# Attention and a gelu MLP on one core: q and k of batches 2 to 7 loaded by the casting DMA of GpSimd and transposed in 64-column tiles

## The chip, the core and the metric

The kernel runs on one core of a Trainium2 chip. The metric is the device time of one execution in microseconds, taken as the median of several runs. Beside it, one execution was recorded by the hardware profiler; its span (first to last instruction) is somewhat shorter than its time. The engines are named as in the profile: PE is TensorE's matmul, PEld its weight load, DVE is VectorE, ACT is ScalarE, POOL is GpSimd, SP is SyncE.

## What is computed

The inputs q, k and v have the shape (8 batches, 12 heads, 448 positions, 64); w_in is 768 x 2048 and w_out 2048 x 768. All are float32, and so is the output (3584 x 768).

```python
def _attn_ref(q, k, v) -> np.ndarray:
    S = q.shape[2]
    scale = 1.0 / np.sqrt(q.shape[-1])
    scores = scale * np.matmul(q, k.transpose(0, 1, 3, 2))
    attn = np.maximum(scores, 0.0) ** 2 / S
    return np.matmul(attn, v).astype(np.float32)

def _moe_ref(x, w_in, w_out) -> np.ndarray:
    h = x @ w_in
    g = h * (1.0 / (1.0 + np.exp(-1.702 * h)))
    return (g @ w_out).astype(np.float32)
...
    attn_out = _attn_ref(**attn_kwargs)
    B, H, S, D = attn_out.shape
    x = np.ascontiguousarray(attn_out.transpose(0, 2, 1, 3)).reshape(B * S, H * D)
    return _moe_ref(x=x, **moe_kwargs)
```

## The kernel before

All matmuls run in float16 with float32 sums. The work is cut as follows.

**Attention.** A unit is four heads of one batch: 24 units, three to a batch. For each unit the kernel needs q and k with the head dimension on the partitions (tiles qT and kT), so both are transposed by PE into a PSUM bank and copied out. The scores of a unit come in seven steps of four matmuls each, on 64*64 tiles of PE, into two PSUM banks; a relu on ACT or DVE brings each bank into a tile `at`, a square on ACT or DVE follows in place, and 28 matmuls on 64*64 tiles multiply `at` with v. Their two banks are copied into xb, the input of the MLP.

**MLP.** The product with w_in is done directly for batch 0 (2 matmuls of 448 columns a step). For batches 1 to 7 it is done by Winograd's form of Strassen's scheme with seven products instead of eight (6 matmuls of 224 columns a step), with sums of blocks of w_in (winS) and of xb (T) made by DVE. The result passes through float32 tiles `gf`: a gelu on ACT writes a gf tile, and a widening step on POOL or DVE turns it into float16 in `ring`, which holds the hidden layer of two batches. The product with w_out uses the same seven-product scheme over pairs of 128-token tiles (8 matmuls of 384 columns a step); sums of ring go to `asum`, those of w_out to wT. The results go through `osb` to the output by SP's queue.

**Loads.** v, w_in and w_out, and q and k of units 1 to 5, are loaded by DMAs that GpSimd issues and that convert float32 to float16 on the way (`load_cast`, L98). q and k of unit 0 and of units 6 to 23 are loaded as float32 by SP (`load`, L94) into the tiles qst and kst, of which there is one each, and converted by a copy on POOL, ACT or DVE (`cast`, L103); that copy also lays the columns out in blocks of 128, two heads side by side. Tiles k16 and q16 hold the float16 forms, two buffers each.

**Transposes.** `trans_pe` (L112) has two forms. If the tile was laid out by `cast`, a tensor takes 7 transposes of 128 columns (L117, tile shape 128*128). If it came from `load_cast`, the two halves lie apart, and a tensor takes 14 transposes of 64 columns, with outputs on partitions 0 to 63 and 64 to 127 (L122, tile shape 128*64).

**The order** is written out by hand. A long string of words gives the order of all operations; each engine executes its own in that order, one after another, each waiting for what it needs. A word is a name, its numbers, an optional PSUM bank list after `@`, and an optional engine after `:` (a for ACT, d for DVE, p for POOL). The words used in this text are: `Lq6` (SP load of q of unit 6), `Q6`, `K6` (conversion), `jq1`, `jk1` (casting load by POOL), `V3` (casting load of v of unit 3), `jwa0`, `jwb0` (the two halves of the first piece of w_in), `jo1.0` (a quarter of w_out), `tq6`, `tk6` (transposes), `eq6`, `ek6` (copy out of PSUM), `s5.5` (scores of unit 5, step 5), `r5.5.1` (relu of its second bank, on ACT unless marked), `x5.5` (square, on DVE unless marked), `a5` (product with v), `e5.0` (copy to xb), `f0.4.1` (first product of batch 0, block 4, second of three steps), `g0.4` (its gelu, on ACT), `v0.4` (its widening, on POOL unless marked), `u1.0.0`, `t`, `b` (products, copies and sums of batches 1 to 7), `p`, `h`, `l` (second product and its results), `W`, `S`, `T`, `A` (sums of w_out, w_in, xb and ring), `o` and `q` with numbers (stores), `G3` (a small DMA on SP that waits for the last piece of w_in, L384) and `z` (matmuls on zeros, zp, while the first loads are under way). Default engines stand in this line:

```python
        home = {"K": "a", "Q": "p", "r": "a", "t": "a", "h": "a", "v": "p"}
```

The pools that matter here have these numbers of buffers: k16 and q16 two each, v16 four, gf five, osb three. The eight PSUM banks are named by number in the words, so a step waits until the earlier content of its banks has been read.

Of the kernel before, what the change touches and what calls it, by code (L numbers as in the profile page):

```python
# [8 lines left out]
F32 = mybir.dt.float32  # L9
# [6 lines left out]
def kernel(  # L16
# [31 lines left out]
    for name, bufs in (("cst", 1), ("kst", 1), ("qst", 1), ("k16", 2), ("q16", 2), ("v16", 4),  # L48
                       ("kT", 3), ("qT", 3), ("at", 15), ("xb", 2),
                       ("T1", 1), ("T2", 1), ("T4", 1), ("gf", 5),  # L50
                       ("as0", 1), ("as1", 1), ("osb", 3)):
        pool(name, bufs)
# [10 lines left out]
    gate = const("gate", [1, 64])  # L63
# [30 lines left out]
    def load(n, u):  # L94
        units[u][n + "st"] = new(f"{n}st", [128, 2, S], F32)
        nc.sync.dma_start(out=units[u][n + "st"], in_=quad(n, u))
# [287 lines left out]
    def sp_gate(e, p, i):  # L384
        nc.sync.dma_start(out=gate[0:1, :], in_=win[i][127:128, 0, 0:64])

    with tc.manual_schedule():
# [4 lines left out]
               "G": sp_gate,  # L392
# [29 lines left out]
        def zeros(e, p, n):  # L422
# [8 lines left out]
            "Lq0 Lk0 z9@0 jq1 jk1 I V0 V1 z1 Q0:d z1 z1 z1 z1 z1 z1 tq0@1 K0:d eq0:a tk0@2 ek0 "  # L431
            "tq1@3 jk2 eq1 s0.1@4.5 jq2 s0.4@6.7 s0.5@0.1 r0.1.1 r0.1.0:d s0.0@2.3 jq3 r0.5.1 "
            "r0.5.0:d s0.6@5.4 r0.0.0 r0.0.1:d r0.6.0 s0.2@1.0 x0.5 r0.2.0 s0.3@2.3 tk1@5 r0.2.1 "
            "x0.1 r0.4.0 ek1 jk3 r0.3.0 x0.2 r0.6.1 s1.6@1.0 jwb0 s1.3@6.5 r0.3.1:d r1.6.0 jwa0 "
            "r1.6.1 x0.6 s1.2@2.4 s1.0@3.1 r1.3.0 x0.3 r1.2.0 s1.5@0.6 x0.0 r0.4.1 r1.5.0:d r1.2.1 "
            "s1.1@2.7 r1.0.1 r1.0.0:d tk2@0 r1.1.0 x0.4 s1.4@4.1 r1.3.1 tq2@3 ek2 r1.1.1 a0@2.5 jq4 "
            "eq2 x1.3:a x1.2 jk4 r1.5.1 r1.4.0:d tq3@0 e0.0:a V2 x1.0 s2.3@7.3 e0.1:a tk3@6 jwb2 "
            "eq3 r2.3.1 s2.2@4.2 r1.4.1 ek3 s2.1@5.0 jwa2 r2.3.0 x1.1 s3.3@3.1 r2.1.1 jwa1 s2.4@6.7 "
            "x1.6 r2.2.0 jwb1 x1.4 r3.3.1 x1.5 a1@0.4 r2.1.0 jk5 r2.4.1 r3.3.0:d r2.2.1 jq5 "
            "s2.0@1.5 r2.4.0:d s3.2@7.3 e1.1:a f0.1.0@2 V3 e1.0 r2.0.0 s2.5@6.4 r2.0.1 r3.2.1:d "  # L440
            "jwb3 s3.4@0.1 r3.2.0 f0.1.1 r2.5.1:d r2.5.0 f0.0.0@5 jwa3 x2.2 f0.0.1 r3.4.0 V4 x2.0 "
            "s2.6@3.7 r3.4.1 s3.0@4.6 r2.6.0 x2.1 tk4@0 V5 r3.0.1 f0.2.0@1 r3.0.0:d r2.6.1 jo0.0 "
# [12 lines left out]
            "x5.3 V6 f0.12.0@1 r5.6.1 K6:d f0.14.0@5 v0.4 r5.2.1 f0.12.1 r5.6.0:d Lk7 x5.0:a "
            "u1.1.0@3 x5.1 u1.0.0@2 r5.2.0 x5.6 r5.4.0 f0.13.0@0 x5.5 u1.2.0@7 e4.1:a S3.1 x5.2:a "
            "f0.12.2 x5.4 f0.14.1 g0.12 a5@4.6 S3.3 Q6:d S1.2 Lq8 tq6@1 e5.0:a v0.12:d f0.13.1 T1.1 "
            "e5.1:a f0.14.2 t1.1.0:d tk6@4 g0.14 T1.2 f0.13.2 S0.3 u1.0.1@6 g0.13 S3.2 p0.0@5 "
            "t1.0.0 v0.13 eq6:a b1.0.1 v0.14 S1.4 u1.0.2 ek6:a S3.4 u1.1.1@0 g1.0.1 T1.3 u1.3.0@1 "
            "t1.0.2 b1.1.1 v1.0.1 u1.1.2 S1.3 g1.1.1 u1.0.4 W0.1 t1.1.2 u1.0.3 W2.1 t1.0.4 u1.1.4 "  # L460
            "K7 b1.0.3 u1.1.3 W1.1 g1.0.3 Lk8 f0.9.0@4 T1.4 t1.1.4 u1.0.6 v1.0.3 Q8:a b1.1.3 f0.9.1 "
            "v1.1.1 f0.9.2 b1.0.6 Lq7 u1.1.6 W3.1 g0.9 u1.3.1@6 g1.1.3 b1.1.6 v0.9 t1.2.0 u1.1.5 "
            "v1.1.3:d t1.3.0 A0.1@0 u1.2.1@4 g1.0.6 W2.3 u1.2.2 g1.1.6 v1.0.6 b1.2.1 tk7@0 t1.2.2 "
            "u1.0.5 b1.3.1 v1.1.6 W1.3 u1.3.2 g1.3.1 W0.3 g1.2.1 u1.2.4 v1.3.1 W3.2 t1.3.2 u1.3.3 "
            "t1.2.4 u1.2.3 A0.2@1 ek7:a u1.2.5 W3.3 g1.0.5 b1.2.3 u1.3.4 K8 v1.0.5 h0.0:d tq8@0 "
            "W2.2 u1.2.6 g1.2.5 Lk9 W1.2 eq8:a p0.1@2 v1.2.5 b1.2.6 W0.2 t1.3.4 v1.2.1 W2.4 "
            "s6.0@7.0 p0.2 r6.0.0 Q7 l0.1 g1.1.5 b1.3.3 r6.0.1 V8 s6.4@4.7 Lq9 W0.4 h0.2 s6.2@3.0 "
            "p0.3 A0.3 r6.2.0 r6.4.1 W3.4 r6.2.1 W1.4 r6.4.0 s6.5@3.7 v1.1.5:d tq7@0 r6.5.0 A0.4 "
            "p0.4 r6.5.1 eq7 x6.2:a x6.5 s6.6@4.3 x6.0 h0.4 s6.3@7.0 Q9 r6.6.1 u1.3.5 r6.3.1:d "
            "r6.3.0 tk8@3 l0.3 g1.3.5 p0.5 K9:p Lq10 r6.6.0:d x6.4:a ek8 v1.3.5 Lk11 x6.3:a "  # L470
            "s7.4@0.7 l0.5 s6.1@1.4 u1.3.6 r7.4.0 r6.1.1:d o1 r7.4.1 x6.6 s7.0@3.5 s7.1@0.4 r6.1.0 "
            "p0.6 b1.3.6 r7.0.1 x6.1 r7.1.0 r7.0.0 x7.4 s7.3@7.1 r7.1.1 s7.2@6.5 l0.6 a6@0.3 r7.2.0 "
            "x7.1 o0 r7.3.0 A2.1@0 r7.2.1 s7.6@4.2 x7.0 r7.3.1 s8.4@6.7 V10 tq9@5 r7.6.0 r7.6.1:d "
            "tk9@1 Q10 e6.1:a r8.4.0:d p2.0@4 eq9:a ek9 K11:p r8.4.1:d x7.2:a s8.2@2.3 x7.6 "
            "s7.5@6.5 Lk10 p2.1@1 r7.5.1 r7.5.0:d Lq11 e6.0:a x7.3 x7.5:a r8.2.0:d s8.1@7.5 a7@6.0 "
            "r8.2.1:d r8.1.1 r8.1.0 A2.2@1 h2.0 x8.1 s8.6@2.3 s8.3@5.7 e7.0:a p2.2 r8.3.0:d e7.1:a "
            "K10:p r8.6.0 r8.6.1:d r8.3.1 l2.1 V13 s9.0@6.5 Lk12 x8.6:a s8.0@0.2 x8.3 s8.5@3.7 p2.3 "
            "r8.0.0:d r8.0.1 r9.0.1 x8.2 r8.5.1 x8.0 tk11@0 r8.5.0 u2.1.0@2 x8.4 ek11:a x8.5 a8@5.7 "
# [152 lines left out]
```

## Time and profile before

| | |
|---|---|
| median of 3 runs | 374.8 us (373.97 to 374.81) |
| profiled execution | 374.8 us, span 373.0 us |
| mean granted clock | 0.998 |
| busy share of the span | PE 98%, PEld 68%, DVE 86%, ACT 80%, POOL 31% |
| chain that ended last | PE 95%, DVE 3%, ACT 1% |
| DMA bytes | 43.16 MB, mean 116 GB/s |
| DMA queue of SP | 28.06 MB, 25.7% of 16 engines |
| DMA queue of POOL | 14.09 MB, 25.2% of 16 engines |
| landing of an SP load of q or k (448 KB) | median 4.5 and 4.2 us |
| landing of a POOL load of q or k (224 KB written) | median 5.9 and 5.4 us |

The page gives busy time per engine, then the span in 40 slices, the DMA queues, the chain of work that ended last (followed back from the last instruction to what released each step), the costliest groups of instructions with the idle time ahead of them and what ended it, and the DMA issues. A group line reads: source line, engine, operation, output and inputs, tile shape of PE, sizes, number of instructions, busy us, mean ns of one, idle us ahead and the releaser. A timeline line reads: start us, us, engine, line, operation, tiles, sizes, number, and in brackets the idle time before it and what ended it. PE's matmuls overlap, so the time that one really takes is the distance between the starts of two.

### The profile page before, as it was taken

How to read it: one execution, taken by the hardware profiler on the slowest of the kernel's cores; microseconds unless marked ns; L12 is line 12 of the kernel's file. 1: busy time of each engine (PE TensorE's matmuls, PEld its weight loads, DVE VectorE, ACT ScalarE, POOL GpSimd, SP SyncE). 2: the span in 40 equal slices, each digit the busy share in tenths (PEclk: the TensorE clock that was granted, in tenths of full speed). 3: DMA queues.
4: the chain of work that ended last, by engine and by line, in shares of the span. 5: the costliest groups of instructions: out<-in, count | busy, mean ns of one | idle time of the engine just before them, and what ended most of it. 6: DMA issues, size and time to landing. Idle time of an engine off the chain costs nothing.

```text
span 373.0 us, 9514 instructions
## 1 busy us (share of the span) xinstructions
PE 365.6 (98%) x3830; PEld 252.9 (68%) x3830; DVE 321.5 (86%) x602; ACT 297.3 (80%) x568; POOL 114.3 (31%) x164
## 2 busy tenths in 40 slices
PE   8899999999999999999999999999999999999995
PEld 4444568855589555886568965599568855788663
DVE  3999999999999998898899699978998889767762
ACT  3999989999988999789978997899994897636310
POOL 6464523452334424231341322335400410012000
PEclk9999999999999999999999999999999999999999
DMA  9999999357673437360572524620520301110344
GB/s 195 171 188 206 238 232 232 135 138 203 166 196 99 120 62 209 112 160 2 134 199 34 177 28 114 183 37 2 95 43 2 86 2 41 45 44 16 71 99 114
DMA packets 31981, 43.16 MB, mean 116 GB/s; under 512 B 2368, under 2 KB 28608, under 8 KB 31936
## 3 DMA queue, kind: packets, MB, share of 16 engines
q1 hardware_dynamic: 14928, 28.06, 25.7%
q0 software_dynamic: 16608, 14.09, 25.2%
q8 instruction: 30, 0.49, 0.5%
q10 hardware_dynamic: 400, 0.39, 0.4%
q14 instruction: 15, 0.12, 0.1%
HBM read 45.61 MB, written 11.01 MB: 152 GB/s over the span
## 4 chain that ended last, share of the span: by engine, by line
PE 95%; DVE 3%; ACT 1%; issue 0%
PE ox L188 35%; PE hx L188 30%; PE sc L141 10%; PE av L172 8%; PE ht L208 5%; PE tr L117 4%; PE zp L426 1%; DVE at L85 1%; DVE at L152 1%; PE tr L122 1%; ACT at L154 1%; DVE kT L80 0%; DVE qT L80 0%; DVE osb L357 0%; DVE wT L417 0%
## 5 line engine op out<-in xcount | busy, mean ns | idle before, releaser
L154 ACT ACTIVATE at<-sc 128x448 f16<-128x448 f32 x229 | 112.2, 567 | 10.6 <-PE sc L141 9.9
L198 POOL TENSOR_SCALAR ring<-gf 128x448 f16<-128x448 f32 x87 | 53.7, 617 | 151.0 <-ACT gf L195 144.0
L188 PE MATMUL ox<-wout,ring 128*128 128x384 f16 x448 | 80.3, 326 | 0.0
L188 PEld LDWEIGHTS <-ring 128*128 128x128 f16 x568 | 53.0, 98 | 37.5 <-issue 7.6
L152 DVE TENSOR_SCALAR at<-sc 128x448 f16<-128x448 f32 x107 | 63.9, 617 | 5.8 <-PE sc L141 5.6
L85 DVE TENSOR_TENSOR at<-at 128x896 f16<-128x896 f16 x107 | 65.5, 636 | 1.7 <-ACT at L154 1.6
L188 PEld LDWEIGHTS <-win 128*128 128x128 f16 x672 | 63.8, 98 | 4.4 <-issue 2.1
L85 DVE TENSOR_TENSOR gf<-hx,gf 128x448 f32<-128x448 f32 x84 | 50.8, 620 | 9.9 <-PE hx L188 5.2
L160 ACT ACTIVATE at<-at 128x896 f16<-128x896 f16 x61 | 57.7, 960 | 0.5
L188 PE MATMUL hx<-xb,win 128*128 128x224 f16 x504 | 57.0, 259 | 0.0
L195 ACT ACTIVATE gf<-gf 128x448 f32<-128x448 f32 x84 | 47.2, 578 | 11.5 <-DVE gf L85 11.3
L141 PE MATMUL sc<-qT,kT 64*64 64x448 f16 x672 | 50.2, 359 | 1.6 <-DVE kT L80 1.1
L188 PEld LDWEIGHTS <-winS 128*128 128x128 f16 x504 | 48.0, 98 | 3.1 <-issue 1.3
L76 ACT ACTIVATE gf<-hx 128x448 f32<-128x448 f32 x60 | 31.8, 541 | 13.4 <-PE hx L188 11.4
L188 PE MATMUL ox<-wT,asum 128*128 128x384 f16 x224 | 40.6, 327 | 0.0
L188 PE MATMUL hx<-T,winS 128*128 128x224 f16 x336 | 39.7, 259 | 0.0
L172 PE MATMUL av<-at,v 64*64 64x448 f16 x672 | 36.2, 350 | 0.1
L141 PEld LDWEIGHTS <-kT 64*64 64x64 f16 x672 | 17.1, 105 | 23.9 <-issue 17.3
L188 PEld LDWEIGHTS <-asum 128*128 128x128 f16 x224 | 20.8, 98 | 16.6 <-issue 3.4
L357 DVE SCALAR_TENSOR_TENSOR osb<-ox,osb 128x384 f32<-128x384 f32 (+1 forms) x44 | 23.8, 541 | 5.9 <-PE ox L188 5.7
L78 ACT ACTIVATE osb<-ox 128x384 f32<-128x384 f32 x26 | 13.1, 503 | 19.6 <-PE ox L188 16.8
L172 PEld LDWEIGHTS <-v 64*64 64x64 f16 x672 | 20.4, 107 | 11.6 <-issue 1.5
(61 smaller groups left out, 426.0 us busy)
## 6 DMA issues: line engine op xcount, KB each, us to landing
out_dram<-osb SPq DMA_DIRECT2D x52, 192.0 KB, 3.0
qst<-in_q_dram SPq DMA_DIRECT2D x19, 448.0 KB, 4.5
kst<-in_k_dram SPq DMA_DIRECT2D x19, 448.0 KB, 4.2
v<-in_v_dram POOLq DMA_DIRECT2D x24, 224.0 KB, 5.0
win<-in_moe_w_in_dram POOLq DMA_DIRECT2D x8, 384.0 KB, 9.7
wout<-in_moe_w_out_dram POOLq DMA_DIRECT2D x4, 768.0 KB, 20.6
q<-in_q_dram POOLq DMA_DIRECT2D x5, 224.0 KB, 5.9
k<-in_k_dram POOLq DMA_DIRECT2D x5, 224.0 KB, 5.4
```

The source lines that it names most:

```text
L76: nc.scalar.activation(out=o, in_=i, func=AF.Copy)
L85: eng[e].tensor_tensor(out=o, in0=x, in1=y, op=op)
L141: nc.tensor.matmul(out=sc[a][c, 0:S], lhsT=st["kT"][r, j, c], rhs=st["qT"][r, :, c], start=True, stop=True)
L152: nc.vector.tensor_scalar(out=o, in0=i, scalar1=0.0, scalar2=None, op0=ALU.max)
L154: nc.scalar.activation(out=o, in_=i, func=AF.Relu)
L160: nc.scalar.activation(out=at, in_=at, func=AF.Square)
L172: nc.tensor.matmul(out=av[s][64 * a:64 * a + 64, 0:S], lhsT=v16[r, a, 64 * j:64 * j + 64], rhs=at[r, a, :], start=(j == 0), stop=(j == J - 1))
L188: nc.tensor.matmul(out=o, lhsT=lhs(i), rhs=rhs(i), start=start and i == 0, stop=i == n - 1, skip_group_check=True)
L195: nc.scalar.activation(out=o, in_=i, func=AF.Gelu_apprx_sigmoid, scale=1.0 / SC)
L198: eng[e].tensor_scalar(out=o, in0=i, scalar1=SC, scalar2=1.0, op0=ALU.mult, op1=ALU.mult)
L208: nc.tensor.matmul(out=hp[g, f][:, 0:S], lhsT=w[:, i, fo:fo + 128], rhs=xts[g][:, i, :], start=i == 0, stop=i == NK - 1)
L357: nc.vector.scalar_tensor_tensor(out=o, in0=x, scalar=1.0 / SC, in1=o, op0=ALU.mult, op1=ALU.add)
```

## The change

q and k of units 6 to 23 (batches 2 to 7) are no longer loaded by SP as float32 and converted. They are loaded by POOL's casting DMA, as those of units 1 to 5 were, and are transposed in the 64-column form. Only unit 0 keeps the float32 load, now into a piece of `ring` that is not yet in use. The tiles qst and kst go, k16 and q16 have four buffers each, and G3 with its tile goes. All operations stand in a new order; the number of every other operation stays the same, and a few steps change between ACT, DVE and POOL. In the diff only the beginning of the two orders is shown, up to the first Strassen steps of batch 1.

```diff
@@ -45,7 +45,7 @@
     def pool(name, bufs, **kw):
         pools[name] = ctx.enter_context(tc.tile_pool(name=name, bufs=bufs, **kw))
 
-    for name, bufs in (("cst", 1), ("kst", 1), ("qst", 1), ("k16", 2), ("q16", 2), ("v16", 4),
+    for name, bufs in (("cst", 1), ("k16", 4), ("q16", 4), ("v16", 4),
                        ("kT", 3), ("qT", 3), ("at", 15), ("xb", 2),
                        ("T1", 1), ("T2", 1), ("T4", 1), ("gf", 5),
                        ("as0", 1), ("as1", 1), ("osb", 3)):
@@ -60,7 +60,6 @@
         return pools["cst"].tile(shape, dt, name=name)
 
     ident = const("ident", [128, 128])
-    gate = const("gate", [1, 64])
     warm = const("warm", [1, 1], F32)
     win = [const(f"win{i}", [128, NK, WQ * 128]) for i in range(NF // WQ)]
     winS = [[const(f"winS{i}_{n}", [128, HK, 256]) for n in range(3)] for i in range(NF // WQ)]
@@ -92,7 +91,9 @@
         return src[n][b].rearrange("(a i s) (p j) d -> i (s p) a (j d)", a=2, i=NP, j=J)[pr]
 
     def load(n, u):
-        units[u][n + "st"] = new(f"{n}st", [128, 2, S], F32)
+        o = "kq".index(n) * 4 * S
+        x = ring.rearrange("p f c -> p (f c)")[:, o:o + 4 * S].bitcast(F32)
+        units[u][n + "st"] = x.rearrange("p (a c) -> p a c", a=2)
         nc.sync.dma_start(out=units[u][n + "st"], in_=quad(n, u))
 
     def load_cast(n, u):
@@ -381,15 +382,11 @@
             in_=moe_w_out[i * WO * 128:(i + 1) * WO * 128, h * NOUT:(h + 1) * NOUT].rearrange(
                 "(f p) d -> p f d", p=128))
 
-    def sp_gate(e, p, i):
-        nc.sync.dma_start(out=gate[0:1, :], in_=win[i][127:128, 0, 0:64])
-
     with tc.manual_schedule():
         two = {"S": s_sum, "W": w_sum, "T": t_sum, "s": scores, "r": relu, "x": square,
                "e": xt_evac, "f": m1, "o": store, "u": unit_product,
                "t": unit_snap, "b": unit_add, "A": a_sum, "p": pair_product, "h": pair_snap,
                "l": pair_last, "q": store_part, "jo": load_w_out, "a": attn_v,
-               "G": sp_gate,
                "I": lambda e, p: make_identity(nc, ident),
                "jwa": lambda e, p, i: load_w_in(0, i), "jwb": lambda e, p, i: load_w_in(1, i),
                "V": lambda e, p, u: load_cast("v", u)}
@@ -428,175 +425,172 @@
 
         two["z"] = zeros
         words = (
-            "Lq0 Lk0 z9@0 jq1 jk1 I V0 V1 z1 Q0:d z1 z1 z1 z1 z1 z1 tq0@1 K0:d eq0:a tk0@2 ek0 "
-            "tq1@3 jk2 eq1 s0.1@4.5 jq2 s0.4@6.7 s0.5@0.1 r0.1.1 r0.1.0:d s0.0@2.3 jq3 r0.5.1 "
-            "r0.5.0:d s0.6@5.4 r0.0.0 r0.0.1:d r0.6.0 s0.2@1.0 x0.5 r0.2.0 s0.3@2.3 tk1@5 r0.2.1 "
-            "x0.1 r0.4.0 ek1 jk3 r0.3.0 x0.2 r0.6.1 s1.6@1.0 jwb0 s1.3@6.5 r0.3.1:d r1.6.0 jwa0 "
-            "r1.6.1 x0.6 s1.2@2.4 s1.0@3.1 r1.3.0 x0.3 r1.2.0 s1.5@0.6 x0.0 r0.4.1 r1.5.0:d r1.2.1 "
-            "s1.1@2.7 r1.0.1 r1.0.0:d tk2@0 r1.1.0 x0.4 s1.4@4.1 r1.3.1 tq2@3 ek2 r1.1.1 a0@2.5 jq4 "
-            "eq2 x1.3:a x1.2 jk4 r1.5.1 r1.4.0:d tq3@0 e0.0:a V2 x1.0 s2.3@7.3 e0.1:a tk3@6 jwb2 "
-            "eq3 r2.3.1 s2.2@4.2 r1.4.1 ek3 s2.1@5.0 jwa2 r2.3.0 x1.1 s3.3@3.1 r2.1.1 jwa1 s2.4@6.7 "
-            "x1.6 r2.2.0 jwb1 x1.4 r3.3.1 x1.5 a1@0.4 r2.1.0 jk5 r2.4.1 r3.3.0:d r2.2.1 jq5 "
-            "s2.0@1.5 r2.4.0:d s3.2@7.3 e1.1:a f0.1.0@2 V3 e1.0 r2.0.0 s2.5@6.4 r2.0.1 r3.2.1:d "
-            "jwb3 s3.4@0.1 r3.2.0 f0.1.1 r2.5.1:d r2.5.0 f0.0.0@5 jwa3 x2.2 f0.0.1 r3.4.0 V4 x2.0 "
-            "s2.6@3.7 r3.4.1 s3.0@4.6 r2.6.0 x2.1 tk4@0 V5 r3.0.1 f0.2.0@1 r3.0.0:d r2.6.1 jo0.0 "
-            "f0.2.1 x2.3 x2.5:a s3.6@3.6 x2.4 x2.6 a2@4.7 jo1.0 r3.6.0 r3.6.1 jo1.1 x3.4 tq4@3 ek4 "
-            "e2.0:a jo0.1 f0.3.0@6 e2.1:a x3.0 f0.3.1 x3.2:a S0.1 f0.0.2 V14 f0.3.2 S0.2 g0.0 "
-            "f0.1.2 eq4 g0.3 f0.2.2 g0.1 x3.3 s3.1@0.4 v0.3 s4.3@7.5 g0.2 s4.1@3.6 v0.1:d f0.10.0@2 "
-            "r4.1.1 f0.10.1 r3.1.1:d r4.3.0 f0.10.2 r3.1.0 v0.0:d f0.8.0@1 r4.3.1 f0.8.1 x3.1 g0.10 "
-            "f0.8.2 v0.2:d r4.1.0 s4.6@6.4 S2.1 v0.10 s4.5@7.0 s3.5@5.2 r4.5.0:d r4.5.1 f0.4.0@3 "
-            "g0.8 f0.4.1 r4.6.0:d f0.6.0@7 x3.6:a v0.8:d f0.4.2 r3.5.1:d f0.6.1 r4.6.1 x4.5 f0.6.2 "
-            "r3.5.0 x4.1 tq5@0 g0.4 tk5@1 x3.5 g0.6 s4.2@6.2 eq5:a ek5 s4.4@4.5 a3@3.7 r4.4.1:d "
-            "r4.2.0 G3 x4.3 r4.2.1 Lk6 s4.0@0.1 S1.1 s5.0@5.6 e3.1:a Lq6 f0.5.0@2 r4.0.0:d r4.4.0 "
...
+            "Lq0 Lk0 z9@0 jq1 jk1 jq2 jk2 jq3 z1 Q0:d z1 z1 I z1 z1 z1 z1 V0 tq0@1 K0:d eq0:a jwa0 "
+            "tk0@2 jk3 ek0 tq1@3 eq1 V1 s0.4@4.5 s0.2@6.7 s0.0@0.1 r0.4.0 r0.4.1:d s0.6@2.3 jq4 "
+            "r0.2.0 r0.0.1:d s0.5@4.5 r0.2.1 jwb0 x0.4 r0.5.0 s0.1@6.1 tk1@7 r0.6.1:d r0.1.0 V2 "
+            "tq2@4 r0.6.0 x0.2 jk4 s0.3@3.6 r0.1.1 ek1 r0.5.1 jwa2 eq2 r0.0.0 s1.6@2.1 s1.0@7.5 "
+            "r0.3.0:d r1.6.0 jq5 s1.1@4.0 r1.6.1 x0.0 tk2@3 jwb2 r1.0.0 r1.0.1:d s1.2@2.1 r1.1.1 "
+            "jwb1 ek2 r0.3.1 tq3@7 x0.6 r1.2.1 jk5 s1.4@5.0 s1.5@3.6 r1.1.0 r1.4.1:d jwa1 r1.5.1 "
+            "r1.4.0:d s1.3@1.4 x0.1:a V3 x1.0 x0.3 x0.5 a0@0.6 r1.2.0 jwb3 r1.5.0 jwa3 eq3:a x1.2 "
+            "s2.3@5.2 x1.4 r1.3.0 V4 s2.5@3.7 e0.0:a r1.3.1:d tk3@1 e0.1:a jo0.0 x1.1 s2.2@0.4 "
+            "r2.3.0 ek3 r2.5.0 s2.4@6.5 x1.6 x1.3:a x1.5 a1@1.3 r2.4.0 r2.4.1:d r2.3.1 r2.2.0:d "
+            "r2.2.1 s2.0@6.5 V5 e1.0 f0.1.0@2 e1.1:a s2.6@0.4 r2.5.1 r2.0.1:d s3.3@1.3 jq6 r2.6.1 "
+            "f0.1.1 r2.0.0:d r3.3.0 f0.0.0@7 jo1.0 x2.4 r2.6.0 s2.1@5.4 s3.4@6.1 x2.2 r2.1.0 jo1.1 "
+            "f0.0.1 r2.1.1 r3.3.1:d f0.3.0@0 f0.3.1 r3.4.0 jk6 x2.1 r3.4.1 s3.0@5.4 s3.2@3.6 x2.0 "
+            "jq8 r3.0.1 tq4@1 r3.2.0:d r3.2.1 tk4@4 jo0.1 x2.5:a x2.3 x2.6 a2@3.6 jk7 r3.0.0 ek4 "
+            "eq4:a jq7 f0.2.0@5 e2.1 f0.2.1 e2.0:a V6 x3.4 s4.5@4.1 s3.6@6.3 r4.5.0:d r4.5.1 f0.3.2 "
+            "r3.6.0 f0.2.2 r3.6.1:d f0.0.2 g0.3 x3.0 f0.1.2 g0.2 s4.3@4.1 g0.0 s4.1@6.3 v0.2 "
+            "s3.5@0.5 r4.3.0:d r4.1.0 f0.8.0@7 v0.0 r4.1.1:d r3.5.1 f0.8.1 f0.10.0@4 g0.1 jk8 x4.1 "
+            "f0.8.2 x3.6:a S0.1 f0.10.1 f0.10.2 x3.2 r3.5.0 s4.0@6.3 v0.3:d r4.3.1 s3.1@5.2 "
+            "r4.0.0:d tk5@0 r3.1.1 tq5@1 g0.10 ek5 f0.6.0@6 r3.1.0 S2.1 f0.6.1 g0.8 x3.3 f0.6.2 "
+            "r4.0.1 f0.4.0@2 v0.8 eq5 x3.1:a f0.4.1 x3.5 jk9 f0.4.2 x4.0 s4.2@4.0 g0.4 s4.6@5.7 jq9 "
+            "a3@3.1 S2.2 g0.6 v0.4 r4.2.0:d r4.2.1 r4.6.1 v0.10 s5.5@2.6 s5.0@4.0 e3.1 r5.5.1 v0.6 "
+            "f0.7.0@7 r5.0.1:d r5.5.0 f0.7.1 v0.1 f0.7.2 e3.0:a r5.0.0:d r4.6.0 s4.4@1.6 V8 S1.1 "
+            "s5.4@0.2 s5.1@3.4 r4.4.0 x4.2 f0.12.0@5 r4.4.1 f0.15.0@1 x4.6 g0.7 f0.12.1 x4.4 r5.4.0 "
+            "f0.12.2 r5.1.1 S1.2 f0.15.1 r5.1.0 f0.11.0@6 S2.4 f0.15.2 x4.3:a r5.4.1:d f0.11.1 S1.3 "
+            "f0.11.2 g0.12 f0.14.0@7 x4.5 g0.15 s5.3@0.4 x5.1 a4@3.2 v0.15 r5.3.1 S3.1 g0.11 v0.12 "
+            "r5.3.0 s5.6@5.1 S3.2 s5.2@4.6 f0.5.0@0 v0.11 r5.2.1 r5.6.1:d f0.5.1 r5.2.0 f0.13.0@6 "
+            "x5.3 V7 e4.0:a f0.5.2 x5.4 x5.2:a f0.14.1 r5.6.0:d u1.0.0@1 x5.0:a S0.2 u1.1.0@4 S3.3 "
+            "f0.13.1 x5.5:a x5.6 a5@3.5 v0.7:d e4.1:a S1.4 g0.5 t1.1.0:d tq6@2 v0.5 e5.0:a T1.1 "
...
```

## The prediction

> **What bounds the kernel now.** I read the page first, then busy time by stretches, the chain of waits in order of time, TensorE's groups with shapes kept apart, and GpSimd's and ScalarE's timelines where the first transfers crowd.
>
> The page's busy times, then two stretches (columns: us, busy us of PE, PEld, DVE, ACT and POOL with instruction counts, clock, DMA share, GB/s):
>
> ```profile
> PE 365.6 (98%) x3830; PEld 252.9 (68%) x3830; DVE 321.5 (86%) x602; ACT 297.3 (80%) x568; POOL 114.3 (31%) x164
> ```
> ```profile
> 0.00:23.00 23.00, 20.19 (x255) 10.85 (x256) 17.22 (x34) 17.08 (x36) 14.36 (x26) 1.00 1.07 183
> 23.00:60.00 37.00, 37.00 (x412) 21.12 (x413) 35.41 (x70) 34.89 (x71) 15.15 (x21) 1.00 1.24 223
> ```
>
> PE never rests from 23 us on: its start-to-start times sum to the span there. So every nanosecond added to PE's stream after 23 us is added to the kernel, and every wait of PE too; freed DVE, ACT or POOL time is worth nothing by itself. Note the DMA share above 1 until 60 us: the 16 DMA engines are full all that while.
>
> Pieces of the chain (start us, us, what), and the two transpose forms (the last figures: busy us, mean ns, idle):
>
> ```profile
> 37.88 0.90 PE tr L122 x28
> ...
> 72.46 1.30 PE ox L188 x8
> 74.07 1.41 PE ox L188 x8
> ...
> 123.68 0.78 PE tr L117 x14
> ```
> ```profile
> L117 PE MATMUL tr<-ident,q 128*128 128x128 f16 x133 | 10.6, 219 | 0.0
> L122 PE MATMUL tr<-ident,q 128*64 128x128 f16 x70 | 2.9, 222 | 0.0
> ```
>
> A tensor turned by 7 full-width transposes (L117) takes 0.39 us; by 14 of 64 columns (L122), 28 to 30 ns apart, 0.415 us, plus something when the next work has another tile shape. The same 8 matmuls take 1.30 us when the next work also uses 128*128 tiles and 1.41 when it is a score (64*64). Start to start over all steps, a change of tile shape costs 0.094 us.
>
> GpSimd, 24 to 40 us, then ScalarE's gelus into gf in those us:
>
> ```profile
> 24.14 0.68 POOL L375 DMA_DIRECT2D win<-in_moe_w_in_dram  x1 [0.49 <-DMA v<-in_v_dram]
> 27.00 0.66 POOL L375 DMA_DIRECT2D win<-in_moe_w_in_dram  x1 [2.18 <-DMA win<-in_moe_w_in_dram]
> 28.90 0.71 POOL L100 DMA_DIRECT2D v<-in_v_dram  x1 [1.24 <-DMA win<-in_moe_w_in_dram]
> ...
> 36.72 0.88 POOL L379 DMA_DIRECT2D wout<-in_moe_w_out_dram  x1 [0.22 <-issue]
> 38.79 0.70 POOL L100 DMA_DIRECT2D v<-in_v_dram  x1 [1.20 <-PE tr L122]
> 39.56 1.46 POOL L198 TENSOR_SCALAR ring<-gf 128x448 f16<-128x448 f32 x2
> ```
> ```profile
> 35.83 0.54 ACT L195 ACTIVATE gf<-ht 128x448 f32<-128x448 f32 x1
> ...
> 37.94 1.00 ACT L195 ACTIVATE gf<-ht 128x448 f32<-128x448 f32 x2
> ```
>
> The issue of a casting DMA waits for an earlier one to land. In the trace the 22nd to the 29th were issued at 27.00, 28.90, 30.88, 32.64, 34.75, 35.62, 36.72, 38.79; the 14th to the 21st landed at 26.72, 28.61, 30.35, 32.35, 34.47, 35.10, 36.43, 38.26. So eight may be under way: number n goes about 0.3 us after number n-8 has landed, and all that stands behind it on POOL waits too. The first widen of batch 0 on POOL (v0.3), placed among PE steps of 32 us, therefore ran at 39.56. It cost nothing: v0.1, v0.0, v0.2 and v0.8 are on DVE, and the gelus g0.8, g0.4, g0.6 (35.83, 37.94 and after) found free gf buffers without POOL.
>
> **The change part by part.** *Transposes.* 36 tensors go from L117 to L122: 36 x (0.415 - 0.391) = 0.9 us. *Order.* Walking both orders, PE changes tile shape 136 times before and 151 times after (the new order puts 20 pairs of transposes back to back, but they now differ from everything around them): 15 x 0.094 = 1.4 us. All other PE steps are the same in number and shape. So PE gains 2.3 us; bounds: 0.9 if no change of shape were added, 4.3 if each tensor took the 0.51 us of the chain's single pieces. Counted with these durations from f0.1.0 (22.93 us in before) PE would end at 366.3 before (it really ended at 368.4) and 369.1 after: 2.9 us, of which 0.5 is work that the new order puts behind f0.1.0.
>
> A rule of the Trainium skill speaks against the 64-column form: "TensorEngine Tiling", Restrictions, says that column tiling turns fast weight load off, and "TensorE: Matmul & The Clock Gate", LDWEIGHTS, prices a load at its columns over 1.2 GHz, 53 ns for 64; were these loads the limit, a tensor would take an estimated 0.75 us and the change cost 13 us on PE. The trace has 28 to 30 ns between these transposes, so the loads overlap, and the row is used.
>
> *Casts.* 36 casts go: on POOL 12 of 1.145 and 13 of 0.976 us (26.4), on ACT 7 of 0.95 (6.7), on DVE 4 of about 0.65 (2.6). POOL gets 36 more issues at 0.75 (27.0), so its sum is unchanged. ACT and DVE are not the bound after 23 us; taken at nothing, hidden under PE's unbroken stream. What this could at most return is the 2.1 us that PE loses in before against its own count. *SP* loses 36 loads and the gate behind win3; its stores no longer queue with loads: nothing waits for them. *Landing.* A cast load took 5.4 to 5.9 us against 4.2 to 4.5; after batch 1 each stands at least 11 us of PE work ahead of its transpose. Nothing.
>
> *Head.* Up to f0.1.0 ACT has 15.6 us of work after and 16.1 before, DVE 16.0 in both, and both are busy almost without a gap from 8.3 us: no change. The identity is now behind five issues (1.26 + 0.89 + 4 x 0.72 = 5.0, ready 5.6), still before tq0 at 6.20.
>
> *What POOL is held up by.* This is the large term. Before the first widen the new order has 34 casting DMAs instead of 29: V6 is the 34th, and waits for the 26th. The first 21 of before are, but for their order, in the first 26 of after, with five more: a w_in piece (384 KB, 2.0 us between landings), V4 and V5 (1.15 each), jo0.0 (a w_out quarter, 768 KB) and jq6 (1.17). For w_out I take 3.8: twice w_in is 4.0; four of them with four SP loads (1.57 each) took from 42.32 to 63.24, giving 3.65. With the 1.65 us that before lost between its 4th and 5th landing to a two-deep buffer, the 26th lands at 38.26 + 2.0 + 2.3 + 3.8 + 1.2 - 1.65 = 45.9. V6 goes at 46.2 and ends at 46.9; v0.2 ends at 47.5, v0.0 at 48.1 (0.6 each). Then k8 waits for jo1.0 (49.7), so v0.8 ends at 51.3; k9 for jo1.1 (53.5), q9 for jk6 (54.7), ending at 55.7; then v0.4, v0.10, v0.6, v0.1 end at 56.3, 56.9, 57.5, 58.1.
>
> Now only one early widen is on DVE (v0.3). gf has five buffers: g0.3, g0.2, g0.0, g0.1, g0.10 take them, g0.8 gets v0.3's, g0.4 must have v0.2's and g0.6 v0.0's. ACT, in order, stands at g0.4 until 47.5, with r4.2.1, r4.6.1 and the rest queued behind. PE's count reaches s5.5 at 40.7; its banks 2 and 6 come free with g0.4 and g0.6, at 48.7: 8.0 us lost. Then g0.7 takes v0.8's buffer in time, but g0.12, g0.15, g0.11 need v0.4, v0.10, v0.6 (56.3, 56.9, 57.5); s5.6 needs the banks of the first two, s5.2 that of the third, and f0.5.0 the relu r5.3.0 behind them, at about 58.9 where the count says 49.0. Lag 9.9 us. By then the w_out quarters have landed (the last about 60) and no later DMA is that long; PE, the bound, gives nothing back. If POOL's landings are 2 us earlier, the lag is some 7; if gf were handed out in strict rotation, g0.7 would wait for v0.1 and f0.5.0 come at 63.5, lag 14.5.
>
> *Clock.* The opening 16 zp matmuls (128x384) took 5.24 us, 0.32 apart, where the same width later takes 0.163: a PE that was idle starts at half pace. An 8 us rest may bring that back, for 0 to 2.6 us. From 48.7 to 57.5 PE has 7.8 us of work in 8.8, so at most 1.6 would show. I take 0. The skill's clock page ("TensorE: Matmul & The Clock Gate", Part 1: The HAM clock gate) puts the drop after about 3.4 us of idleness and the recovery at as much, so by it an estimated 1.7 us would be lost and at most 0.7 show.
>
> Sum, against the profiled execution (374.8 us, span 373.0; also the median): 374.8 + 2.9 + 9.9 = 387.6.
>
> **The rivals.** (a) *POOL is not held up where it hurts*: the gelus find buffers, and only PE's 2.9 us remain: 377.7 (376.3 to 379). For it: before lived with a POOL 8 us late. Against it: then four of the first six widens were on DVE, now one. (b) *Strict rotation of gf* and the half clock: 374.8 + 2.9 + 14.5 = 392.2, to 393.8. Against it: in before g0.6 did not wait for v0.3. (c) *Faster, by the head*: PE takes 16.7 us from tq0 to f0.1.0 for 11.2 us of work. POOL waited 2.4, 1.6 and 3.4 us there for its two k16 and q16 buffers; with four, tensors come earlier. If that returned 5 us and POOL's lateness hurt nobody, 374.8 + 2.9 - 5 = 372.7; it decides if f0.1.0 starts before 20.0 us. Against it: ACT and DVE have no gap there for it to close.
>
> **How the numbers follow.** Held up as worked out, 383 to 393: 0.66. Held up for less (lag 2 to 5, 379 to 383): 0.09. (a): 0.14. (b): 0.05. (c): 0.06. The range leaves out the upper end of (b), (c) and the lower part of (a): 377.0 to 392.5. About 0.3% (1.1 us) is what a measurement of this kernel can tell. Faster by more than that: (c), 0.06; within it: the lowest of (a), 0.03; slower: 0.91.
>
> **What would show it.** Right: 644 transposes of form 128*64 at about 30 ns and 28 of the other; POOL's waits name wout and k DMAs between 38 and 56 us, its first widen ends near 47.5; ACT's gelu waits for POOL's ring widen; PE has a hole of some 8 us near 41 and a second, shorter one near 57; the rest as before, PE's last matmul near 381. Wrong: a first POOL widen near 40, or gelus that pass it; PE without a hole; transposes above 50 ns apart; f0.1.0 moved by more than 2 us.

## The result, and the profile after

The changed kernel takes 386.69 us, the median of three runs (385.88 to 386.87). The ratio to the kernel before, 374.8 us, is 1.0319, with a 95% interval of 1.0288 to 1.035. The forecast was 387.6 us, slower. The profiled execution took 386.87 us with a span of 385.1 us.

The page's busy times come first, then the same two stretches as before and a finer cut of the second one. The columns of a stretch are us, busy us of PE, PEld, DVE, ACT and POOL with instruction counts, granted clock, DMA share and GB/s.

```profile
PE 370.5 (96%) x4082; PEld 254.1 (66%) x4082; DVE 326.1 (85%) x610; ACT 287.5 (75%) x551; POOL 114.5 (30%) x173
```
```profile
0.00:23.00 23.00, 20.19 (x256) 10.95 (x256) 17.49 (x34) 17.39 (x35) 15.05 (x27) 1.00 1.12 201
23.00:60.00 37.00, 29.01 (x306) 13.53 (x299) 25.81 (x47) 25.13 (x52) 17.90 (x25) 0.86 1.29 203
```
```profile
23.00:41.00 18.00, 17.48 (x218) 8.73 (x211) 16.81 (x32) 15.18 (x31) 8.09 (x11) 1.00 1.28 202
41.00:48.30 7.30, 0.00 (x0) 0.00 (x0) 0.17 (x1) 0.55 (x1) 3.31 (x6) 0.65 1.30 203
48.30:60.00 11.70, 11.53 (x88) 4.80 (x88) 8.82 (x15) 9.41 (x20) 6.50 (x10) 0.78 1.30 204
60.00:106.00 46.00, 46.00 (x541) 31.89 (x540) 44.51 (x86) 40.00 (x79) 18.31 (x26) 1.00 0.55 88
```

The first 23 us and everything from 60 us on look as they did: PE is never at rest from there. Between 23 and 60 us PE starts 306 matmuls where it started 412. For 7.3 us it starts none, while DVE and ACT stand almost still too and the DMA engines stay full. What works in those 7.3 us are the transfers and POOL.

More than a few steps changed their engine with the new order: some 360 of the 1100 steps for which the order chooses among ACT, DVE and POOL, nearly as many one way as the other. Among them are seven widens of batch 0 (v0.0, v0.1, v0.2, v0.6, v0.8, v0.11, v0.12) that went from DVE to POOL. As the experiments show, the slowdown comes from these together with the loads, not from the loads alone.

GpSimd's timeline and then ScalarE's, where the loads crowd (start us, us, engine, line, operation, tiles, number; in brackets the idle time ahead and what ended it):

```profile
43.78 0.70 POOL L101 DMA_DIRECT2D k<-in_k_dram  x1 [2.67 <-DMA wout<-in_moe_w_out_dram]
45.22 0.70 POOL L101 DMA_DIRECT2D q<-in_q_dram  x1 [0.74 <-DMA v<-in_v_dram]
46.33 0.70 POOL L101 DMA_DIRECT2D v<-in_v_dram  x1 [0.41 <-issue]
47.11 1.21 POOL L199 TENSOR_SCALAR ring<-gf 128x448 f16<-128x448 f32 x2
```
```profile
47.71 1.19 ACT L196 ACTIVATE gf<-ht 128x448 f32<-128x448 f32 x2 [9.14 <-POOL ring L199]
...
56.92 0.54 ACT L196 ACTIVATE gf<-ht 128x448 f32<-128x448 f32 x1 [0.48 <-POOL ring L199]
```

POOL's first two widens run from 47.11 to 48.32, behind the issue of V6, as forecast (v0.2 done at 47.5, v0.0 at 48.1). ScalarE stands for 9.14 us at g0.4 until a gf buffer is widened. The line of 56.92 is the forecast's second, shorter hold-up, at g0.12 (then g0.15 and g0.11). TensorE, in the next fence, waits 7.80 us for g0.4 and g0.6 to free the banks of s5.5:

```profile
39.00 1.49 PE L173 MATMUL av<-at,v 64*64 64x448 f16 x28
48.30 1.67 PE L142 MATMUL sc<-qT,kT 64*64 64x448 f16 x8 [7.80 <-ACT gf L196]
49.90 2.42 PE L209 MATMUL ht<-xb,win 128*128 128x448 f16 x6
```

The chain of waits puts the same stretch down to a transfer. It has a piece there that the chain of before did not have, the landing of a v tile (V5), which the issue of jq7 at 45.22 waited for:

```profile
30.91 13.78 DMA v<-in_v_dram
```

The transposes, by form (the last figures: busy us, mean ns, idle us):

```profile
L123 PE MATMUL tr<-ident,q 128*64 128x128 f16 x322 | 13.0, 220 | 0.1
L118 PE MATMUL tr<-ident,q 128*128 128x128 f16 x7 | 0.6, 219 | 0.0
```

With those of k that is 644 of the 64-column form, as forecast, still 0.415 us from a tensor's first transpose to the next step of the same tile shape. The forecast's 28 of full width is a wrong count: unit 0 has two tensors of 7, so there are 14. No term of the sum rests on it.

### The profile page after: what moved, and what is told of

It reads as the page before. It is cut to its first block, busy times and chain, and to the rows that moved or that the text cites. A ratio compares the mean times of both kernels' runs of the same rounds, so it can differ in the third digit from the quotient of the medians.

```text
span 385.1 us, 9956 instructions
## 1 busy us (share of the span) xinstructions
PE 370.5 (96%) x4082; PEld 254.1 (66%) x4082; DVE 326.1 (85%) x610; ACT 287.5 (75%) x551; POOL 114.5 (30%) x173
## 3 DMA queue, kind: packets, MB, share of 16 engines
q0 software_dynamic: 26400, 22.35, 39.6%
## 4 chain that ended last, share of the span: by engine, by line
PE 89%; ACT 4%; DMA 4%; DVE 1%; issue 1%; POOL 0%; POOLq 0%
PE ox L189 34%; PE hx L189 30%; PE sc L142 9%; PE av L173 7%; PE tr L123 5%; DMA v<-in_v_dram 4%; ACT at L155 3%; PE ht L209 3%; PE zp L423 1%; DVE at L84 1%; ACT at L161 0%; POOL ring L199 0%; ACT gf L196 0%; DVE winS L84 0%; ACT qT L75 0%
## 5 line engine op out<-in xcount | busy, mean ns | idle before, releaser
L155 ACT ACTIVATE at<-sc 128x448 f16<-128x448 f32 x230 | 113.5, 567 | 11.9 <-PE sc L142 11.3
L153 DVE TENSOR_SCALAR at<-sc 128x448 f16<-128x448 f32 x106 | 62.9, 617 | 13.3 <-PE sc L142 12.9
L84 DVE TENSOR_TENSOR at<-at 128x896 f16<-128x896 f16 x108 | 67.2, 639 | 2.3 <-ACT at L155 1.4
L142 PE MATMUL sc<-qT,kT 64*64 64x448 f16 x672 | 51.6, 365 | 9.0 <-ACT gf L196 7.8
L142 PEld LDWEIGHTS <-kT 64*64 64x64 f16 x672 | 18.0, 106 | 32.9 <-issue 26.4
L173 PE MATMUL av<-at,v 64*64 64x448 f16 x672 | 37.0, 350 | 0.5 <-ACT at L161 0.5
L101 POOL DMA_DIRECT2D v<-in_v_dram x24 | 17.3, 721 | 37.4 <-PE sc L142 31.4
```

Of the source, the lines that this page charges most:

```text
L84: eng[e].tensor_tensor(out=o, in0=x, in1=y, op=op)
L142: nc.tensor.matmul(out=sc[a][c, 0:S], lhsT=st["kT"][r, j, c], rhs=st["qT"][r, :, c], start=True, stop=True)
L153: nc.vector.tensor_scalar(out=o, in0=i, scalar1=0.0, scalar2=None, op0=ALU.max)
L155: nc.scalar.activation(out=o, in_=i, func=AF.Relu)
L173: nc.tensor.matmul(out=av[s][64 * a:64 * a + 64, 0:S], lhsT=v16[r, a, 64 * j:64 * j + 64], rhs=at[r, a, :], start=(j == 0), stop=(j == J - 1))
```

## The experiments

The first four ran together on one chip, beside a kernel before of 375.12 us (374.23 to 375.41). They take the two parts of the slowdown apart: POOL's lateness and PE's dearer transposes.

**The ten early widens on DVE.** The order of the changed kernel is kept, and POOL's queue with all its loads; only ten widens of batch 0 leave it.

```diff
-  ... v0.2 ... v0.0 ... v0.8 ... v0.4 ... v0.10 ... v0.6 ... v0.1 ... v0.15 ... v0.12 ... v0.11
+  ... v0.2:d ... v0.0:d ... v0.8:d ... v0.4:d ... v0.10:d ... v0.6:d ... v0.1:d ... v0.15:d ... v0.12:d ... v0.11:d
```

> The changed kernel with ten early widens of batch 0 (v0.2, v0.0, v0.8, v0.4, v0.10, v0.6, v0.1, v0.15, v0.12, v0.11) on DVE instead of POOL; every load, its place and PE's stream stay. Theory (widens stand behind waiting DMAs on POOL): the hole of 8 us near 41 us goes, and the second near 57. PE's own count gives 377.7; DVE takes on ten widens of about 0.4 us where it was 95% busy, of which 0 to 4 us may show: 379.5 us expected, 377.5 to 382. Rival (the loads land too late for PE, or the transposes are dear): nothing of that changes, 385 to 387.

Measured: 378.47 us (377.92 to 378.62), ratio 1.0089 (1.0074 to 1.0104). POOL's timeline shows that the loads are as late as ever, and the waits of ScalarE for POOL's widens (us in all, count, longest) have gone from 12.4 us, the longest 9.1, to next to nothing:

```profile
42.67 0.70 POOL L101 DMA_DIRECT2D k<-in_k_dram  x1 [2.97 <-DMA wout<-in_moe_w_out_dram]
...
45.83 0.70 POOL L101 DMA_DIRECT2D v<-in_v_dram  x1 [1.03 <-PE ht L209]
```
```profile
ACT gf L196 <- POOL ring L199: 2.4, 5, 0.8
```

So the late loads by themselves hurt nobody. What costs is that widens stand behind them in POOL's queue.

**The loads behind the widens.** The other way round: the widens stay on POOL, and eight loads of units 6 to 9 move behind them.

```diff
-  ... jk6 ... jq8 ... jk7 ... jq7 ... V6 ... jk8 ... jk9 ... jq9 ... v0.1 ... V7 ... v1.0.5
+  ... v0.1 V6 ... V7 jk6 ... v1.0.1 jk7 ... v1.1.1 jq8 ... v0.13 jq7 ... v1.0.3 jk8 ... v1.1.3 jk9 ... v1.0.5 jq9
```

> The changed kernel with eight casting loads (V6, k6, q8, k7, q7, k8, k9, q9) moved in the order behind the early widens of batch 0; engines and PE's stream stay. Theory: the first widen on POOL is then behind 29 casting DMAs as in the kernel before, runs near 38 us, and ACT does not stand: 377.9 us, 376.8 to 379.5. Rival (DVE and ACT were short of time in the new order, or the transposes cost 8 us or more): 384 or more.

Measured: 378.96 us (378.16 to 379.11), ratio 1.0101 (1.0084 to 1.0118), 1.1 us above what was expected. POOL's first widen now runs here:

```profile
37.92 2.25 POOL L199 TENSOR_SCALAR ring<-gf 128x448 f16<-128x448 f32 x3
```

The long hole is gone without any help from DVE. Four small ones remain in PE's stream, of 1.11 us (a3), 0.65 (s5.5), 0.88 (u1.2.4) and 0.48 (tk7), which the expectation did not have. Two edits that have nothing in common but the order of widens and loads on POOL each take about 8 us away.

**The kernel before, transposed in 64-column tiles.** Order, loads and conversions are those of before; the converted tensors of units 6 to 23 are turned by 14 transposes.

```diff
-            if len(x.shape) == 2:
+            if len(x.shape) == 2 and u == 0:
...
+                w = (x[:, a, 64 * j:64 * j + 64] if len(x.shape) == 3
+                     else x[:, 128 * j + 64 * a:128 * j + 64 * a + 64])
...
-                    lhsT=x[:, a, 64 * j:64 * j + 64], rhs=ident[:, :], is_transpose=True)
+                    lhsT=w, rhs=ident[:, :], is_transpose=True)
```

> The kernel before with one thing changed: q and k of units 6 to 23 are transposed in 14 pieces of 64 columns (tile shape 128*64) instead of 7 of 128; loads, conversions and order stay. By the count of the trace before, 36 x 0.024 us and 47 more changes of tile shape (183 against 136) x 0.094 us: +5.3, 380.1 us expected, 379 to 381. Rival by the weight-load rule (53 ns for each of 504 loads): +13 or more, 388. Rival that changes of shape hide: +0.9, 375.7.

Measured: 380.39 us (380.33 to 380.59), ratio 1.0144 (1.0129 to 1.0159): 5.27 us above before, where the count says 5.3. The page's busy line has PE at work for 5.6 us more than before's 365.6, and for the same share of the span, so this is PE's own work:

```profile
PE 371.2 (98%) x4082; PEld 251.5 (66%) x4082; DVE 324.6 (86%) x602; ACT 298.4 (79%) x568; POOL 112.2 (30%) x164
```

In before's order the 64-column form raises the changes of tile shape from 136 to 183, and these 47 at 0.094 us make 4.4 of the 5.3 us. The new order, with its pairs of transposes back to back, has only 151. The Trainium skill's rule on the lost fast weight load ("TensorEngine Tiling", Restrictions), priced by "TensorE: Matmul & The Clock Gate", LDWEIGHTS, would by an estimate have made this run some 13 us slower; the measured 5.27 us speak against it.

**The kernel before with the cast loads.** Before's order again, with the 64-column form, and now also with POOL's casting loads in the places of SP's; the conversions and G3 go, and k16 and q16 have four buffers. The first two new loads, q6 and k6, stand between the w_out pieces; they alone of the new loads come ahead of the first widen.

```diff
-  ... Lk6 ... Lq6 ... K6:d ... Q6:d ... Lq8 ... K7 ...
+  ... jo1.0 jq6 jo1.1 jk6 ... jq8 ...
```

> The order of the kernel before with the loads of the change: q and k of units 6 to 23 by POOL's casting DMA into four buffers each, at the places of the SP loads (q6 and k6 moved up between the w_out quarters), the conversions and the gate gone, 64-column transposes. PE's stream is that of the kernel before with 64-column transposes. Theory: in this order four of the first six widens are on DVE, so the two more DMAs ahead of the first POOL widen hurt nobody, and the time is that of the kernel before with 64-column transposes within 1 us: 380, 379 to 381.5. Rival (the casting loads themselves cost the time, in any order): 8 us or more above that kernel, 388.

Measured: 379.24 us (379.02 to 379.7), ratio 1.0111 (1.0094 to 1.0128). POOL's first widen is about 1 us later than before's 39.56, and PE has no hole:

```profile
40.70 1.49 POOL L202 TENSOR_SCALAR ring<-gf 128x448 f16<-128x448 f32 x2
```

It takes 1.15 us less than the run before it (0.63 in the two profiled executions). That is all that the freed conversions return, net of what the new loads cost; the dearer transposes cost more than four times as much. Little of it reaches PE: its last matmul ends at 374.07 us, against 374.03 in the run before. From f0.1.0 on PE is 0.6 us quicker, but f0.1.0 comes at 23.32 instead of 22.70. What is left is the end, where 3.8 us follow PE's last matmul instead of 4.5.

The next four ran beside a kernel before of 374.43 us (374.1 to 376.11).

**The changed kernel again.**

> The changed kernel as it is, for a comparison on the same chip as the next three: 386.7 us, 385.5 to 388.

Measured: 386.34 us (386.17 to 386.91), ratio 1.0311 (1.0284 to 1.0338). Its profile shows how far two executions of one kernel differ inside: the landings come some 0.8 us earlier (the 26th at 44.92 us instead of 45.80), the wait ahead of s5.5 is 6.4 us instead of 7.8, and f0.5.0 starts at 59.02 instead of 59.74.

**Two widens on DVE.** Only v0.2 and v0.0, which held g0.4 and g0.6 up. If the loss were the hole at 41 us, this would return nearly all of it.

```diff
-  ... v0.2 ... v0.0 ...
+  ... v0.2:d ... v0.0:d ...
```

> The changed kernel with only the first two POOL widens (v0.2, v0.0) on DVE. Theory (the lag is set by the latest of the absolute times at which POOL gets to its widens, not by the sum of PE's holes): the hole of 8 us before s5.5 goes, but g0.7 then stands until v0.8 (about 51 us) and g0.12, g0.15, g0.11 until v0.4, v0.10, v0.6 (56.5 to 58.6), so f0.5.0 still starts near 59 us (59.7 in the changed kernel) and the time is 386.0, 384.5 to 387. Rival (each hole is a cost of its own): 8 us come back, 378.5.

Measured: 387.56 us (387.09 to 388.11), ratio 1.0341 (1.0313 to 1.037), 1.2 us more than the changed kernel beside it and 0.6 above the expected range. PE's and then ScalarE's timelines show the hole moved to the next widens in POOL's queue:

```profile
51.87 0.91 PE L209 MATMUL ht<-xb,win 128*128 128x448 f16 x2 [5.54 <-ACT gf L196]
```
```profile
51.27 0.54 ACT L196 ACTIVATE gf<-ht 128x448 f32<-128x448 f32 x1 [7.80 <-POOL ring L199]
```

v0.8 is behind jk8, and v0.4 and its neighbours behind jk9 and jq9, as POOL's timeline shows:

```profile
49.90 0.70 POOL L101 DMA_DIRECT2D k<-in_k_dram  x1 [2.90 <-DMA wout<-in_moe_w_out_dram]
50.68 0.56 POOL L199 TENSOR_SCALAR ring<-gf 128x448 f16<-128x448 f32 x1
54.00 0.75 POOL L101 DMA_DIRECT2D k<-in_k_dram  x1 [2.76 <-DMA wout<-in_moe_w_out_dram]
55.17 0.70 POOL L101 DMA_DIRECT2D q<-in_q_dram  x1 [0.42 <-issue]
```

jk8 and jk9 go when the w_out pieces have landed (49.61 and 53.47 us), and jq9 when k6 has (54.63), whatever happened before. f0.5.0 starts at 59.09 (59.74 in the changed kernel). What the end inherits is the clock time of the latest widens, not the sum of the holes ahead of them. Why it then ends later is seen in PE's starts: the five steps after f0.5.0 that lag (f0.13.0 to u1.1.0) come 0.3 to 0.4 us late each, at a granted clock of 0.50 from 60 to 62 us and 0.77 from 62 to 64, and by then nothing hides that. The expectation had no term for this.

**PE kept at work in the hole.** 46 matmuls on zeros, 128x384, into a bank that is free, just ahead of s5.5.

```diff
-            nc.tensor.matmul(out=zp[0][:, ...
+            nc.tensor.matmul(out=zp[-1][:, ...
-  ... v0.10 s5.5@2.6 ...
+  ... v0.10 z46@1 s5.5@2.6 ...
```

> The changed kernel with 46 matmuls on zeros (128x384, about 0.163 us each) ahead of s5.5, where PE rests for 7.8 us. Theory: PE then goes on at full pace, f0.7.0 to f0.7.2 stand 0.38 us apart instead of 0.72, but the end of the lag is set by POOL's widens, so f0.5.0 starts at 59.2 to 59.7 and 0 to 0.6 us come back: 386.4. Rival (the half pace after the rest is a cost of its own, half of 5.2 us): 384.1.

Measured: 386.99 us (386.81 to 388.18), ratio 1.0332 (1.0302 to 1.0363): nothing came back. PE's timeline:

```profile
41.88 7.63 PE L423 MATMUL zp<-wT 128*128 128x384 f16 x46 [0.73 <-DVE xb L79]
49.45 0.57 PE L142 MATMUL sc<-qT,kT 64*64 64x448 f16 x8
49.95 1.31 PE L209 MATMUL ht<-xb,win 128*128 128x448 f16 x6
```

The clock is 1.00 throughout, and the six f0.7 matmuls take 1.31 us instead of 2.42. PE only reaches the next gelu sooner and waits there; f0.5.0 comes at 59.97. So the half pace is real and costs the changed kernel nothing that this run can tell: POOL's later widens set the end.

**The DMA lays the columns out.** If the transposes' price is the form alone, a casting load that already writes blocks of two heads side by side brings the 7 full-width transposes back. On the order of the kernel before with cast loads, units 9 to 23 get two DMAs per tensor; jk9 and jq9 were moved up, behind v1.0.3 and v1.1.1.

```diff
+        if n != "v" and u >= 9:
+            x = new(f"{n}16", [128, J, 2, D], F16)
+            for a in range(2):
+                nc.gpsimd.dma_start(out=x[:, :, a, :], in_=quad(n, u)[:, a, :].rearrange("p (j d) -> p j d", d=D))
+            units[u][n + "16"] = x.rearrange("p j a d -> p (j a d)")
+            return
...
-  ... v1.0.3 ... v1.1.1 ... jk9 ... jq9 ...
+  ... v1.0.3 jk9 ... v1.1.1 jq9 ...
```

> The order of the kernel before with casting loads; for units 9 to 23 the DMA itself lays q and k out in blocks of 128 (two DMAs a tensor, pieces of 64 numbers instead of 448), so that 7 full-width transposes serve and no conversion is needed; units 6 to 8 as in the change. If the small pieces arrive in time, PE's stream is 1.1 us longer than that of the kernel before by count, and up to 1.1 us of small waits come back: 375.0, 373.8 to 376.5. Rival (seven times the pieces hold the DMA queue and POOL up): 380 or more, with POOL waits that name q and k DMAs.

Measured: 379.78 us (379.45 to 380.11), ratio 1.013 (1.0099 to 1.0161), 4.8 us above what was expected and near the rival's 380. PE's count fell as it should, but PE lost 4.6 us between 66 and 76 us. POOL's timeline there, then its group of block loads:

```profile
66.14 2.01 POOL L104 DMA_DIRECT2D q<-in_q_dram  x2
68.15 0.74 POOL L108 DMA_DIRECT2D q<-in_q_dram  x1
68.97 2.53 POOL L208 TENSOR_SCALAR ring<-gf 128x448 f16<-128x448 f32 x3
```
```profile
L104 POOL DMA_DIRECT2D k<-in_k_dram x30 | 29.6, 988 | 0.4
```

The issue of one such DMA takes 0.99 us against 0.74 for a whole tensor in the plain layout, so a tensor costs 2 us of POOL. Three widens of the first seven-product stage stood behind 2.75 us of issues. It is the fault of the change itself, repeated in a new place.

**The same, with those two loads where they were.**

```diff
-  ... v1.0.3 jk9 ... v1.1.1 jq9 ...
+  ... v1.0.3 ... v1.1.1 ...   (jk9 and jq9 after g1.2.5 and s6.4)
```

> As the kernel whose DMA lays out blocks for units 9 to 23, but with the loads of q9 and k9 left at their places of the order before, some 9 us later, instead of among the first widens of the Strassen stage. Theory (there POOL's 2 us of issue for each tensor stood ahead of widens, and 4.6 us were lost between 66 and 76 us): that loss goes, and what remains is the count's 1.1 us for units 6 to 8, less some small waits: 375.3, 374.4 to 376.5. Rival (small pieces cost time everywhere): 379 or more.

Measured, beside a kernel before of 374.61 us (374.02 to 375.33): 376.6 us (376.43 to 377.18), ratio 1.0056 (1.0043 to 1.007), 0.1 us above the expected range. It is the best of the versions with cast loads, and still slower than before. PE waits 3.8 us against its count, 1.7 more than in before; four steps of 0.3 to 0.5 us make most of that. No version here beats the kernel before.

## Why the prediction was right

**PE's own work, +2.9 us: right.** The changed kernel's count from its f0.1.0 to the end is 346.2 us, as worked out. That its two prices hold together is shown in the run of before with 64-column transposes, where they made 5.3 us and 5.27 came; no run has one without the other. The bound of 4.3 from the single pieces of the chain was not needed.

**The casts, nothing: right as a bound, not exactly.** In before's order their removal returned 1.15 us, of which some 0.6 came out of PE's stream, where the prediction saw "at most 2.1". In the changed kernel it can't be told from the hold-up.

**The landings: right to 0.1 us.** The 26th landed at 45.80 (45.9 forecast), jo1.0 at 49.62 (49.7), jo1.1 at 53.47 (53.5), jk6 at 54.66 (54.7). V6 went at 46.33 (46.2). That it is so close is in part luck: in the profile of the changed kernel again the same four landed at 44.92, 48.74, 52.60 and 53.85.

**The mechanism: shown.** Widens off POOL, or loads behind the widens, each remove the long hole. That the widen, not the landing, is what PE waits for is seen in the first of the two, where the landings stayed late.

**The hold-up, 9.9 us: 10.8.** PE ended 12.9 us behind its count, against 2.1 before. f0.5.0, the step that the working followed, came at 59.74, not 58.9, although f0.1.0 came at 22.19, 0.74 us earlier than in before. The mis-sized term is the price of a POOL widen: 0.6 us was taken for each, and the four that began at 55.98 took 0.88 apiece, which puts the end of the third of them, v0.6, at 58.7 instead of 57.5. In the profile of the changed kernel again the four took 0.90 apiece, but began at 55.17, and f0.5.0 came at 59.02; its hold-up by the same sum is 9.6 us. So the price of these widens was too low, while the total of 9.9 lies between those of two executions. POOL's timeline of the changed kernel, and below it that of the run with two widens on DVE, where the same four widens ran:

```profile
55.98 3.52 POOL L199 TENSOR_SCALAR ring<-gf 128x448 f16<-128x448 f32 x4
```
```profile
55.95 2.49 POOL L199 TENSOR_SCALAR ring<-gf 128x448 f16<-128x448 f32 x4
```

**The head, nothing: off by 0.74 us,** in the direction of rival (c). That gain and the 0.9 us of the hold-up cancel: PE's last matmul ended at 381.3 us, the sum said 381.2. In the five other profiles that have this order up to f0.1.0 it comes between 22.00 and 22.84, so how much of the 0.74 is the order's is not shown. What follows PE's end took 3.8 us against 4.6 in before, and that is the 0.7 us by which the profiled execution (386.87) lies under 387.6. It is 3.8 in all the kernels without the SP loads of units 6 to 23 and 4.5 to 4.6 in the two with them; the prediction had no term for it, and its cause stays open.

**The clock, nothing: right,** and shown by the run with PE kept at work. The forecast that at most 1.6 us of it would show was made for a second hole right behind; that hole swallowed it. Where no wait follows, the half pace does cost: some 1.7 us in the run with two widens on DVE.

**The rivals.** (a), 377.7 us, is close to the 378.47 of the run with the widens on DVE: it was wrong on the one point that it turned on. That it is so close is in part luck: in that run PE waits some 2.7 us more against its count than in before, and an f0.1.0 at 22.00 and the shorter end make up for 1.8 of them. (b), strict rotation of gf, is refuted by f0.5.0, which would have come at 63.5. (c) asked for an f0.1.0 before 20.0 us.

That five gf buffers are what couples ScalarE to POOL so tightly was only argued; more of them was not tried.

## What to carry to other kernels

A load that is moved to an engine's queue brings its waits with it: work out when the issue can go (here, when the transfer eight places ahead has landed) and look at everything that stands behind it in that queue. An engine that is busy 30% of the span can hold up one that is busy 98%. Taking away the first hole of such a queue only moves it to the next entry; what counts is when the last of the queued results comes, so move the whole group or none.

## What the runs showed of the hardware

**A widen on POOL is dearer beside some of DVE's work.** In the changed kernel all eight that ran beside no DVE work took 0.556 to 0.567 us. Another 35 of its 85 ran beside DVE work that was not an operation on two SBUF operands (the tiles sc, ht, hx, av, ox and tr lie in PSUM), and they took no more than 0.568. Of the 42 beside such an operation (squares, sums of weights, of xb and of ring), 25 took longer, 0.585 to 1.054. The four at 55.98 took 0.90, 0.82, 0.81 and 0.75, with DVE at squares (at<-at) and sums of w_in without a break. One line of DVE's timeline beside them, and one beside the same four in the run with two widens on DVE, where DVE rested for 3.36 us until 58.20, with 0.56 to 0.57 for each widen:

```profile
56.37 1.88 DVE L84 TENSOR_TENSOR at<-at 128x896 f16<-128x896 f16 x2
```
```profile
58.20 0.62 DVE L153 TENSOR_SCALAR at<-sc 128x448 f16<-128x448 f32 x1 [3.36 <-PE sc L142]
```

The Trainium skill ("SBUF — State Buffer", Who interferes with whom) says that a DVE instruction with two inputs in SBUF contends with a GpSimd instruction that reads SBUF. These lines agree with that, and it goes both ways: the two squares beside these widens took 0.98 and 0.97 us, where 88 squares of the same kernel without a POOL operation beside them took 0.61 to 0.63. No run here was made to test it.

**The clock after a rest.** In the changed kernel the granted clock is 0.50 from 48.3 to 53 us, 0.80 in the next us and 1.00 after it: about 5 us of half pace after a rest of 7.8 us. In the profile of the changed kernel again it is 0.50 from 47.4 to 51 us, 3.6 us after a rest of 6.4. In the run with two widens on DVE it fell to 0.50 a second time, from 59.5 to 62.9 us, after waits of only 1.13 and 0.30 us; PE was busy for 1.87 of the 3.4 us before. The Trainium skill ("TensorE: Matmul & The Clock Gate", Part 1: The HAM clock gate) puts the recovery after at least one window of about 3.4 us of sustained work, and says that these windows run free of the kernel's start; 3.6 and about 5 us agree with that.

**The price of a casting DMA's issue depends on its pieces.** 0.74 us for a tensor of q or k in the plain layout, 0.99 us for half a tensor written in pieces of 64 columns; the queue's packets rose from 26400 in the changed kernel to 72960 for the same 22.35 MB.
